# Slot sums as 512-column matmuls over four token blocks, joined by one small matmul, and a phase rounded by an integer write, in a three-layer attention and soft-MoE kernel

## The chip, the cores and the metric

The kernel runs on one core of a Trainium2 chip. The metric is the device time of one execution in microseconds. A core has TensorE (PE in the profile; its weight loads are PEld), VectorE (DVE), ScalarE (ACT), GpSimd (POOL) and SyncE (SP), which here only issues DMAs. Each engine works through its own instructions in the order in which they were written.

## What is computed

Three layers follow one another. The first is an attention with a 12 by 12 mix of the heads before and after the softmax. The second is `g = h * cos(h)` of `h = x @ w_in`, followed by `g @ w_out`. The third is a soft mixture of experts with 32 slots. The change touches the second layer and the place where it meets the third:

```python
h = x @ w_in                      # x 1792x768, w_in 768x2048
g = h * np.cos(h)
x = g @ w_out                     # never formed by the kernel
logits = x @ phi                  # 1792x32
d = np.exp(logits - logits.max(0)); d /= d.sum(0) + 1e-09
slot_input = d.T @ x              # 32x768
...                               # experts on slot_input, 8 x (768x1024, 1024x768)
c = softmax over slots; out = c @ slot_out
```

The kernel never forms `x` of the third layer. It sums `d.T @ g` (32 slots by 2048 features) and multiplies that sum by `w_out`.

## The kernel before, in words

`phase_a` is the attention, in the order that a planner writes; the change leaves it as it is. `phase_b` is the second layer and the sums over tokens, `phase_c` the experts and the output.

`phase_b` takes the 1792 tokens in four blocks of 512, 512, 512 and 256 (called blocks 0 to 3), and in each block 16 steps of 128 features, 64 steps `v` in all. The function `body(v)` writes one step. `l1` (L699 to L709) puts 18 matmuls on PE that make `h` of 128 features by 512 (or 256) tokens in one of three PSUM buffers. `act` (L716) makes the phase: ACT computes `h / 2 pi + MAGIC` (L718, an Identity with a bias tile, so that the fraction is rounded away), DVE takes MAGIC off again (L719), subtracts the whole turns from `h / 2 pi` (L720), and clears the sign (L722). `split_w` (L647 to L651) divides the weights of a later step in a high part (ACT, L649) and a low part (DVE, L650). Two steps late, `consume` (L738) turns `g` in blocks of 32 by 32 on DVE (L741) into the buffer `gn_all`, and `logits` (L743) puts four matmuls on PE every fourth step. `act2` (L726) is the sine on ACT (L727) and the product on DVE (L728). `load_w` (L640) loads the weights four steps ahead from SP's queue; in block 3 loads for the experts (`ahead`) stand between them in the same queue.

After a block, `soft` (L882) writes the block's share of the softmax into the steps of the next one: `soft0` (L753) copies the logits out, `soft1` (L758) finds the maximum and the exponentials, `soft1_turn` (L783) turns these 32 by 32 into `et`, `soft2` (L787) makes the softmax over slots, and `slots` (L801) adds `d.T @ g`. For every 32 tokens and each half of the features `slots` puts four matmuls on PE, one for each 32 rows `a` of the partitions; each reads 32 rows and 256 columns and writes 32 rows and 256 columns of one of four PSUM buffers `p` (tag "tr"). Four more accumulations stand beside each other in the 32-row strips `c` of each buffer (two for even and odd tokens in each half). A block of 512 tokens takes 128 such matmuls (256 instructions, as an f32 matmul is two), block 3 takes 64. DVE then adds the four buffers to `g_acc` (L818 in block 0, L820 later). For blocks 0 to 2 this stands in the steps of the next block, for block 3 after the last step, where `busy(n)` puts small matmuls without a use between.

`phase_c` begins with `g_acc` [128 by 1024]: 16 matmuls with stacked identities (L997) add the 32-row strips and turn the sum, ACT and DVE copy it to `gT` (L1003, L1001), and 32 matmuls `si` (L1008) multiply it by `w_out`. Then the first expert's matmuls start (`eh`, L1048). 64 units of expert weights of 768 KB go through a ring of 26 buffers: SP issues the load of a later unit when an earlier one has been used (L947). Units 0 to 17 come early; the next ones wait until the steps, `slots` of block 3 and `si` leave their buffers.

Of the kernel before, what the change touches and what calls it, by code (L numbers as in the profile page):

```python
# [9 lines left out]
F32 = mybir.dt.float32  # L10
F32R = mybir.dt.float32r
U32 = mybir.dt.uint32
AF = mybir.ActivationFunctionType
# [586 lines left out]
def phase_b(tc, st, consts, ident, xT_d, w_in, w_out, phi, sums, room, x0, ahead):  # L600
# [9 lines left out]
    with ExitStack() as ctx:  # L610
# [105 lines left out]
        def act(v, h):  # L716
            r = work(v)
            nc.scalar.activation(out=r, in_=h, func=AF.Identity, scale=INV2PI, bias=magic)  # L718
            nc.vector.tensor_scalar(out=r, in0=r, scalar1=MAGIC, scalar2=None, op0=ALU.subtract)  # L719
            nc.vector.scalar_tensor_tensor(out=r, in0=h, scalar=INV2PI, in1=r,  # L720
                                           op0=ALU.mult, op1=ALU.subtract)
            nc.vector.tensor_scalar(out=r.bitcast(U32), in0=r.bitcast(U32), scalar1=0x7FFFFFFF, scalar2=None,  # L722
                                    op0=ALU.bitwise_and)
            return h, r
# [4 lines left out]

        def gn(b, fb):  # L730
            if b == NB - 1:
                x = gn_all[:, 8192 + 1024 * fb:9216 + 1024 * fb]
            else:
                i = (4 * (b + 2 - NB) + fb) % 6
                x = gn_all[:, 2048 * i:2048 * i + 2048]
            return x
# [14 lines left out]
        et, al_t, l4_t = {}, {}, {}  # L751
# [49 lines left out]
        def slots(b):  # L801
            n = SIZES[b]
            pts = [p1.tile([128, 512], F32, tag="tr", bufs=4, name=f"p{b}_{a}")[:, :256] for a in range(4)]
            i = (4 * (b + 2 - NB)) % 6
            for t in range(n // 32):
                for half in range(2):
                    c = 2 * half + t % 2
                    x = 8192 + 2048 * half if b == NB - 1 else 2048 * ((i + 2 * half) % 6)
                    g = gn_all[:, x:x + 8 * n].rearrange("p (f t j) -> p t f j", f=8, j=32)
                    for a in range(4):  # L810
                        r = slice(32 * a, 32 * a + 32)
                        nc.tensor.matmul(pts[a][32 * c:32 * c + 32], et[b][r, 32 * t:32 * t + 32], g[r, t],  # L812
                                         start=(t < 2), stop=(t >= n // 32 - 2))
            out = g_acc.rearrange("p (f a j) -> p a f j", a=4, j=32)
            for a in range(4):
                p = pts[a].rearrange("p (f j) -> p f j", j=32)
                if b == 0:
                    nc.vector.tensor_copy(out=out[:, a], in_=p)  # L818
                else:
                    nc.vector.scalar_tensor_tensor(out=out[:, a], in0=out[:, a], scalar=al_t[b][:, 3:4],  # L820
                                                   in1=p, op0=ALU.mult, op1=ALU.add)
# [60 lines left out]
        def soft(v):  # L882
# [8 lines left out]
            elif b > 0 and f == (3 if b + 1 < NB else 4):  # L891
                slots(b - 1)

# [23 lines left out]
        slots(NB - 1)  # L917
        busy(4)
# [31 lines left out]
def phase_c(tc, ident, cT, g_acc, z_acc, gn_all, x1, cg, w1, w2, st, wo, early, gu, rest, free_x0, out):  # L950
# [5 lines left out]
    with ExitStack() as ctx:  # L956
# [36 lines left out]
        for half in range(2):  # L993
            pt = p1.tile([128, 512], F32, tag="tr", name=f"gtr{half}")
            r = slice(64 * half, 64 * half + 64)
            for k in range(8):
                nc.tensor.matmul(pt[:, 32 * k:32 * k + 32], g_acc[r, 128 * k:128 * k + 128], st[r, :32],  # L997
                                 start=True, stop=True)
            pg = pt[:, :256].rearrange("p (k s) -> p k s", s=32)
            if half:  # L1000
                nc.vector.tensor_copy(out=gT[:, 8:], in_=pg)  # L1001
            else:
                nc.scalar.copy(out=gT[:, :8], in_=pg)  # L1003
# [152 lines left out]
def tile_kernel(ctx: ExitStack, tc: tile.TileContext, q, k, v, w_pre, w_post, w_in, w_out, phi, w1, w2, out):  # L1156
# [4 lines left out]
    with tc.manual_schedule():  # L1161
# [39 lines left out]
        sums.append(pool.tile([128, w_in.shape[1] // 2], F32, name="g_acc"))  # L1201
# [51 lines left out]
```

## Time and profile before

| | us |
|---|---|
| median of 3 runs (range) | 930.11 (929.28 to 931.38) |
| the profiled execution's own time | 931.67 |
| its span | 929.8 |
| PE busy in the span | 874.4 (94%) |
| DVE busy | 643.2 (69%) |
| ACT busy | 521.0 (56%) |
| attention, until the first `h` matmul of PE's long run | 0 to 505 |
| the 64 steps of `phase_b`, first `h` matmul to last | 505 to 806 |
| end of `phase_b` to the first expert matmul | 806 to 832.5 |
| experts and output | 832.5 to 930 |

PE's 94% is a mean of stages with different limits. It holds small matmuls that wait for one another as well as full ones, and in the experts' stage the matmuls wait for weights. So what a change is worth has to be read in its own stage. The granted clock was full in `phase_b`, and between 0.5 and 0.8 of it in some stretches after.

### The profile page before, as it was taken

What the parts mean: (1) busy time and instruction counts of PE and PEld (TensorE: products, weight loads), DVE (VectorE), ACT (ScalarE), POOL (GpSimd) and SP (SyncE); (2) the same over time, 40 slices, a digit from 0 to 9 for tenths busy, and PEclk for the clock granted to TensorE, in tenths of its full rate; (3) what the DMA queues carried; (4) which work ended last, traced back from release to release, by engine and by line L of the source; (5) the groups of instructions that cost most, each with busy time, mean ns of one, the idle gap of its engine ahead of it and who ended that gap; (6) DMA issues with size and microseconds to landing.
All of it is one profiled execution on the core that took longest, in us unless ns stands there. A gap on an engine that the chain in (4) does not pass through costs nothing.

```text
span 929.8 us, 18916 instructions
## 1 busy us (share of the span) xinstructions
PE 874.4 (94%) x7176; PEld 623.6 (67%) x7176; DVE 643.2 (69%) x1348; ACT 521.0 (56%) x1139; POOL 178.8 (19%) x272
## 2 busy tenths in 40 slices
PE   7898999999999999999999999999998989889765
PEld 5556777776777777777778877777776767753212
DVE  4566887778779778778744777887877888823003
ACT  5565777677767678666655644564554546502002
POOL 3232443433434334343300000000000000010000
PEclk9999999999999999999999999999999999989768
DMA  7999797999788997979327732463553467969998
GB/s 166 184 200 216 194 239 214 200 229 261 224 206 224 222 241 180 249 203 248 102 88 249 230 120 68 160 213 110 182 182 126 139 215 215 315 252 414 417 374 291
DMA packets 175478, 198.99 MB, mean 214 GB/s; under 512 B 73424, under 2 KB 147090, under 8 KB 175388
## 3 DMA queue, kind: packets, MB, share of 16 engines
q1 hardware_dynamic: 158504, 159.18, 57.9%
q0 software_dynamic: 14272, 37.96, 18.1%
q8 instruction: 57, 0.93, 0.5%
q10 hardware_dynamic: 2612, 0.65, 0.3%
q14 instruction: 33, 0.27, 0.1%
HBM read 135.40 MB, written 23.59 MB: 171 GB/s over the span
## 4 chain that ended last, share of the span: by engine, by line
PE 75%; DMA 11%; DVE 6%; SPq 3%; ACT 2%; issue 2%; POOL 0%; ACTq 0%; POOLq 0%; DVEq 0%
PE po L443 15%; PE pre L405 14%; PE av L467 8%; PE h L705 7%; PE s L358 7%; PE h L706 7%; PE h L708 7%; DMA early<-in_moe_w_dram 3%; DMA knat<-in_k_dram 3%; PE p L812 2%; DMA cg<-in_moe_w_dram 2%; DMA ring<-in_moe_w_dram 2%; DVE wf L650 2%; PE eh L1048 1%; DMA s<-ss 1%
## 5 line engine op out<-in xcount | busy, mean ns | idle before, releaser
L443 PEld LDWEIGHTS po<-wc,e 120*112 120x112 f32 x1440 | 171.4, 178 | 56.2 <-issue 41.6
L443 PE MATMUL po<-wc,e 120*112 120x120 f32 x1440 | 183.5, 269 | 0.5 <-ACT am L228 0.5
L405 PE MATMUL pre<-s,kron_pre 120*120 120x448 f32 x360 | 168.3, 558 | 5.8 <-issue 3.7
L408 DVE TENSOR_REDUCE mz<-pre 120x1 f32<-120x448 f32 x180 | 111.0, 620 | 49.9 <-PE pre L405 49.0
L378 POOL DMA_DIRECT2D s<-ss x180 | 107.1, 597 | 181.9 <-ACT ss L228 135.5
L705 PE MATMUL h<-x,wh 128*128 128x512 f32 (+1 forms) x384 | 138.7, 371 | 1.3 <-ACT wh L649 1.3
L706 PE MATMUL h<-x,wh 128*128 128x512 f32 (+1 forms) x384 | 135.5, 363 | 0.0
L412 ACT ACTIVATE e<-pre,mz 120x448 f32<-120x448 f32 x180 | 114.5, 637 | 30.8 <-DVE mz L408 28.1
L228 ACT COPY am<-po 112x360 f32<-112x360 f32 x190 | 87.3, 461 | 65.4 <-PE po L443 63.3
L705 PEld LDWEIGHTS h<-x,wh 128*128 128x128 f32 x384 | 72.1, 188 | 24.2 <-ACT cg L718 5.9
L708 PE MATMUL h<-x,wf 128*128 128x512 f32 (+1 forms) x384 | 87.5, 363 | 0.0
L542 POOL TENSOR_TENSOR nar<-nar,cvt 128x384 uint32<-128x384 uint32 x64 | 64.0, 1000 | 98.7 <-DVE cvt L533 42.7
L467 PE MATMUL av<-am,v 112*64 112x120 f32 (+1 forms) x1536 | 83.0, 262 | 0.0
L718 ACT ACTIVATE cg<-h,consts 128x512 f32<-128x512 f32 (+1 forms) x64 | 40.2, 629 | 75.0 <-PE h L708 73.9
L467 PEld LDWEIGHTS av<-am,v 112*64 112x64 f32 x1536 | 74.0, 137 | 10.4 <-issue 5.2
L706 PEld LDWEIGHTS h<-x,wh 128*128 128x128 f32 x384 | 72.2, 188 | 11.3
L708 PEld LDWEIGHTS h<-x,wf 128*128 128x128 f32 x384 | 66.2, 188 | 12.0
L727 ACT ACTIVATE cg<-cg,consts 128x512 f32<-128x512 f32 (+1 forms) x64 | 42.9, 671 | 49.0 <-DVE cg L722 48.8
L1022 POOL MEMSET own<- 128x192 f32 x2 | 0.4, 252 | 361.4 <-PE si L1008 361.4
L405 PEld LDWEIGHTS pre<-s,kron_pre 120*120 120x120 f32 x360 | 54.0, 186 | 23.2 <-issue 17.5
L228 ACT COPY ss<-s 120x448 f32<-120x448 f32 (+1 forms) x104 | 54.1, 532 | 24.9 <-PE s L358 15.6
L650 DVE TENSOR_TENSOR wf<-wf,wh 128x768 fp32r<-128x768 f32 x64 | 60.9, 951 | 9.1 <-ACT wh L649 9.1
(171 smaller groups left out, 1252.8 us busy)
## 6 DMA issues: line engine op xcount, KB each, us to landing
s<-ss POOLq DMA_DIRECT2D x144, 210.0 KB, 7.5
early<-in_moe_w_dram SPq DMA_DIRECT2D x36, 768.0 KB
wf<-w SPq DMA_DIRECT2D x64, 384.0 KB
raw<-in_moe_w_in_dram SPq DMA_DIRECT2D x32, 384.0 KB
w<-nar SPq DMA_DIRECT2D x64, 192.0 KB
raw<-in_moe_w_out_dram SPq DMA_DIRECT2D x32, 384.0 KB
gn<-in_moe_w_dram SPq DMA_DIRECT2D x16, 768.0 KB
early<-w SPq DMA_DIRECT2D x8, 768.0 KB
```

What stands on the lines that cost most here:

```text
L228: nc.scalar.copy(out=out, in_=in_)
L358: nc.tensor.matmul(pts[o][:n, :S], x[r, p, :n], y[r, p, :], start=(i == 0), stop=(i == 2))
L378: QUEUE[e].dma_start(out=s2t[ti][h::12, :n // 10], in_=x[o][:n])
L405: nc.tensor.matmul(prt[gi, c][:, :S], kpre, s2t[ti][:, 3 * g + c, :], start=True, stop=True)
L408: nc.vector.tensor_reduce(out=mz[gi][:, 0, c:c + 1], in_=prt[gi, c][:, :S], axis=AX.X, op=ALU.max, negate=True)
L412: nc.scalar.activation(out=et[gi][:, c, :], in_=prt.pop((gi, c))[:, :S], func=AF.Exp, bias=mz[gi][:, 0, c:c + 1], accum_out=mz[gi][:, 1, c ...
L443: nc.tensor.matmul(pt[:, :360].rearrange("p (g i) -> p g i", i=30)[:, :, 10 * c:10 * c + 10], et[gi][:, c, jt * CJ:(jt + 1) * CJ], wct[gi] ...
L467: nc.tensor.matmul(pt[64 * o:64 * o + 64, x * 120:x * 120 + n], vt[:, g, jt, :], am[ti % 2][:, g, jt, :n], start=(jt == 0), stop=(jt == NJ ...
L650: nc.vector.tensor_tensor(out=wf_t[v], in0=wf_t[v].bitcast(F32), in1=wh.bitcast(F32), op=ALU.subtract)
L705: nc.tensor.matmul(pt, wh[:, c], xh[:, c, :], start=(c == 0), stop=False)
L706: nc.tensor.matmul(pt, wh[:, c], xl[:, c, :], start=False, stop=False)
L708: nc.tensor.matmul(pt, wl[:, c], xh[:, c, :], start=False, stop=(c == 5))
```

## The change

It does four things. The added rows push later code down: L720 of the changed kernel is L718 of the one before, and so on.

1. `act`: ACT multiplies by `1 / 2 pi` and writes a 32-bit integer (Copy, no bias tile). The subtraction on DVE reads that integer, and the instruction that took MAGIC off is gone.
2. `slots`: one matmul covers all 16 x 32 features (512 columns) of its 32 rows, and the strips `c` are four token blocks. A block of 512 tokens takes 64 matmuls, block 3 takes 32. The four full buffers are copied to scratch columns of `gn_all` (block 3: the last one to `cg`), two by ACT, two by DVE.
3. `slots_sum`, new: four matmuls with stacked identities add the strips of each buffer; DVE adds the result to `g_acc`, now [128 by 512], in one instruction (two in block 3). It stands two steps after `slots`; after block 3 right behind it, with four more small matmuls `busy(4)`.
4. `phase_c`: two 32 by 32 turns on DVE make `gT` from `g_acc`. The 16 matmuls and the two copies are gone.

The buffers of `gn` are laid out anew (`HALVES`), so that `slots` can read 16 x 32 features with one pattern.

```diff
         def act(v, h):
             r = work(v)
-            nc.scalar.activation(out=r, in_=h, func=AF.Identity, scale=INV2PI, bias=magic)
-            nc.vector.tensor_scalar(out=r, in0=r, scalar1=MAGIC, scalar2=None, op0=ALU.subtract)
-            nc.vector.scalar_tensor_tensor(out=r, in0=h, scalar=INV2PI, in1=r,
+            i = r.bitcast(I32)
+            nc.scalar.activation(out=i, in_=h, func=AF.Copy, scale=INV2PI)
+            nc.vector.scalar_tensor_tensor(out=r, in0=h, scalar=INV2PI, in1=i,
                                            op0=ALU.mult, op1=ALU.subtract)
...
+        HALVES = [(0, 2), (1, 2), (0, 1)]
+
         def gn(b, fb):
             if b == NB - 1:
-                x = gn_all[:, 8192 + 1024 * fb:9216 + 1024 * fb]
+                return gn_all[:, 8192 + 1024 * fb:9216 + 1024 * fb]
+            x = 4096 * HALVES[b][fb // 2] + 2048 * (fb % 2)
+            return gn_all[:, x:x + 2048]
...
         def slots(b):
             n = SIZES[b]
-            pts = [p1.tile([128, 512], F32, tag="tr", bufs=4, name=f"p{b}_{a}")[:, :256] for a in range(4)]
-            i = (4 * (b + 2 - NB)) % 6
+            pts = [p1.tile([128, 512], F32, tag="tr", bufs=4, name=f"p{b}_{a}") for a in range(4)]
+            g = all_gn(b)
             for t in range(n // 32):
-                for half in range(2):
-                    c = 2 * half + t % 2
-                    x = 8192 + 2048 * half if b == NB - 1 else 2048 * ((i + 2 * half) % 6)
-                    g = gn_all[:, x:x + 8 * n].rearrange("p (f t j) -> p t f j", f=8, j=32)
-                    for a in range(4):
-                        r = slice(32 * a, 32 * a + 32)
-                        nc.tensor.matmul(pts[a][32 * c:32 * c + 32], et[b][r, 32 * t:32 * t + 32], g[r, t],
-                                         start=(t < 2), stop=(t >= n // 32 - 2))
-            out = g_acc.rearrange("p (f a j) -> p a f j", a=4, j=32)
+                c = 32 * (t % 4)
+                for a in range(4):
+                    r = slice(32 * a, 32 * a + 32)
+                    nc.tensor.matmul(pts[a][c:c + 32], et[b][r, 32 * t:32 * t + 32], g[r, t],
+                                     start=(t < 4), stop=(t >= n // 32 - 4))
+            if b + 1 < NB:
+                sc = gn(b, 3)
+                sc_t[b] = [sc[:, 512 * a:512 * a + 512] for a in range(4)]
+            else:
+                sc_t[b] = [gn_all[:, 10752 + 512 * a:11264 + 512 * a] for a in range(3)] + [cg[:, :512]]
             for a in range(4):
-                p = pts[a].rearrange("p (f j) -> p f j", j=32)
-                if b == 0:
-                    nc.vector.tensor_copy(out=out[:, a], in_=p)
+                if a % 2:
+                    nc.vector.tensor_copy(out=sc_t[b][a], in_=pts[a])
                 else:
-                    nc.vector.scalar_tensor_tensor(out=out[:, a], in0=out[:, a], scalar=al_t[b][:, 3:4],
-                                                   in1=p, op0=ALU.mult, op1=ALU.add)
+                    nc.scalar.copy(out=sc_t[b][a], in_=pts[a])
+
+        def slots_sum(b):
+            pt = p1.tile([128, 512], F32, tag="tr", bufs=4, name=f"ps{b}")
+            for a in range(4):
+                nc.tensor.matmul(pt[32 * a:32 * a + 32], st[:, :32], sc_t[b][a], start=True, stop=True)
+            if b == 0:
+                nc.vector.tensor_copy(out=g_acc, in_=pt)
+            else:
+                for c in (slice(0, 512),) if b + 1 < NB else (slice(0, 256), slice(256, 512)):
+                    nc.vector.scalar_tensor_tensor(out=g_acc[:, c], in0=g_acc[:, c], scalar=al_t[b][:, 3:4],
+                                                   in1=pt[:, c], op0=ALU.mult, op1=ALU.add)
...
             elif b > 0 and f == (3 if b + 1 < NB else 4):
                 slots(b - 1)
+            elif b > 0 and f == (5 if b + 1 < NB else 6):
+                slots_sum(b - 1)
...
         slots(NB - 1)
         busy(4)
+        slots_sum(NB - 1)
+        busy(4)
...
         for half in range(2):
-            pt = p1.tile([128, 512], F32, tag="tr", name=f"gtr{half}")
-            r = slice(64 * half, 64 * half + 64)
-            for k in range(8):
-                nc.tensor.matmul(pt[:, 32 * k:32 * k + 32], g_acc[r, 128 * k:128 * k + 128], st[r, :32],
-                                 start=True, stop=True)
-            pg = pt[:, :256].rearrange("p (k s) -> p k s", s=32)
-            if half:
-                nc.vector.tensor_copy(out=gT[:, 8:], in_=pg)
-            else:
-                nc.scalar.copy(out=gT[:, :8], in_=pg)
+            nc.vector.transpose(out=gT[:, 8 * half:8 * half + 8].rearrange("p k s -> p (k s)"),
+                                in_=g_acc[:, 256 * half:256 * half + 256])
```

The order of the instructions changes in three places that matter here. The first is a step of block 3 on DVE. Before, from one turn of `g` to the next:

```order
L741 STREAM_TRANSPOSE gn<-cg 128x256
L728 TENSOR_TENSOR cg<-h_8468,cg 128x256
L719 TENSOR_SCALAR cg<-cg 128x256
L720 SCALAR_TENSOR_TENSOR cg<-h_8498,cg 128x256
L722 TENSOR_SCALAR cg<-cg 128x256
L650 TENSOR_TENSOR wf_5880<-wf_5880,wh_5884 128x768
```

Now, at the same place of DVE's order:

```order
L750 STREAM_TRANSPOSE gn<-cg 128x256
L729 TENSOR_TENSOR cg<-h_8236,cg 128x256
L721 SCALAR_TENSOR_TENSOR cg<-h_8265,cg 128x256
L723 TENSOR_SCALAR cg<-cg 128x256
L651 TENSOR_TENSOR wf_5880<-wf_5880,wh_5884 128x768
```

Five instructions stand where six stood, in all 64 steps. The second place is PE after the last `slots`. Before:

```order
L812 MATMUL p_3_8701<-gn,cg 32x256
L899 MATMUL idle<-ident 128x128 x4
L997 MATMUL gtr_8805<-st,g_acc 128x32 x8
L997 MATMUL gtr_8815<-st,g_acc 128x32 x8
L1008 MATMUL si_8825<-x_5972,gT 32x384 x4
```

Now, on PE from the last `slots` to the first `si`:

```order
L818 MATMUL p_3_8463<-gn,cg 32x512
L920 MATMUL idle<-ident 128x128 x4
L834 MATMUL ps_8504<-gn,st 32x512 x3
L834 MATMUL ps_8504<-cg,st 32x512
L920 MATMUL idle<-ident 128x128 x4
L1023 MATMUL si_8548<-x_5972,gT 32x384 x4
```

The sixteen `gtr` are replaced by four `ps` and four more small ones. The third place is DVE at the same point. Before:

```order
L820 SCALAR_TENSOR_TENSOR g_acc<-g_acc,m_8672,p_0_8698 128x8x32
L820 SCALAR_TENSOR_TENSOR g_acc<-g_acc,m_8672,p_1_8699 128x8x32
L820 SCALAR_TENSOR_TENSOR g_acc<-g_acc,m_8672,p_2_8700 128x8x32
L820 SCALAR_TENSOR_TENSOR g_acc<-g_acc,m_8672,p_3_8701 128x8x32
L991 TENSOR_SCALAR rz<-z_acc 128x1
L992 RECIPROCAL rz<-rz 128x1
L1001 COPY gT<-gtr_8815 128x256
```

Now, on DVE up to the turns that `si` waits for:

```order
L827 COPY gn<-p_1_8461 128x512
L827 COPY cg<-p_3_8463 128x512
L839 SCALAR_TENSOR_TENSOR g_acc<-g_acc,m_8434,ps_8504 128x256 x2
L1014 TENSOR_SCALAR rz<-z_acc 128x1
L1015 RECIPROCAL rz<-rz 128x1
L1017 STREAM_TRANSPOSE gT<-g_acc 128x256 x2
```

DVE now works twice between `slots` and `si`: on the copies ahead of the `ps` matmuls, and on the sums and turns behind them. POOL's and SP's order are as before.

## Rows read from the trace of the kernel before

**Rows 1.** Windows: stretch, its length, each engine's busy us (instructions), clock, DMA.

```profile
636.00:686.00 50.00, 50.00 (x225) 37.80 (x225) 44.44 (x73) 27.04 (x38) 0.00 (x0) 1.00 0.57 186
...
786.00:797.00 11.00, 10.30 (x92) 9.57 (x91) 9.49 (x25) 6.31 (x12) 0.00 (x0) 1.00 0.94 304
797.00:806.00 9.00, 9.00 (x79) 8.37 (x80) 8.79 (x22) 5.47 (x11) 0.00 (x0) 1.00 0.95 302
...
824.00:826.00 2.00, 2.00 (x16) 0.61 (x19) 0.42 (x1) 0.00 (x0) 0.00 (x0) 0.50 1.01 421
...
828.00:830.00 2.00, 2.00 (x32) 0.75 (x28) 0.00 (x0) 0.00 (x0) 0.00 (x0) 1.00 0.03 8
...
846.00:870.00 24.00, 22.65 (x184) 9.47 (x176) 6.19 (x16) 4.74 (x12) 0.39 (x3) 0.93 1.02 415
```

**Rows 2.** Chain that ended last, in block 1: start us, us, what.

```profile
638.08 1.40 PE h L708 x6
642.28 1.40 PE h L708 x6
```

**Rows 3.** Timeline of PE: `slots` of blocks 0, 1, 2: start, us, line, [idle before].

```profile
624.45 5.17 PE L812 MATMUL p<-gn 32*32 32x256 f32 x242 [0.38 <-DVE gn L785]
630.24 0.66 PE L812 MATMUL p<-gn 32*32 32x256 f32 x14 [0.62 <-issue]
...
705.06 3.41 PE L812 MATMUL p<-gn 32*32 32x256 f32 x163 [1.03 <-DVE gn L785]
710.13 2.10 PE L812 MATMUL p<-gn 32*32 32x256 f32 x93 [1.66 <-issue]
...
778.53 4.04 PE L812 MATMUL p<-gn 32*32 32x256 f32 x195 [0.20 <-DVE gn L785]
783.50 1.47 PE L812 MATMUL p<-gn 32*32 32x256 f32 x61 [0.93 <-issue]
```

**Rows 4.** Timeline of DVE, one step of block 3.

```profile
797.70 0.44 DVE L741 STREAM_TRANSPOSE gn<-cg 128x256 f32<-128x256 f32 x1
...
798.07 0.39 DVE L728 TENSOR_TENSOR cg<-h,cg 128x256 f32<-128x256 f32 x1
...
798.37 0.27 DVE L719 TENSOR_SCALAR cg<-cg 128x256 f32<-128x256 f32 x1
...
798.68 0.42 DVE L720 SCALAR_TENSOR_TENSOR cg<-h,cg 128x256 f32<-128x256 f32 x1
...
800.22 0.44 DVE L741 STREAM_TRANSPOSE gn<-cg 128x256 f32<-128x256 f32 x1
```

**Rows 5.** Timeline of DVE behind `slots` of block 2.

```profile
785.33 1.64 DVE L820 SCALAR_TENSOR_TENSOR g_acc<-g_acc,m,p 128x256 f32<-128x256 f32 x4
787.75 0.29 DVE L719 TENSOR_SCALAR cg<-cg 128x256 f32<-128x256 f32 x1 [0.79 <-ACT cg L718]
```

**Rows 6.** Chain, the step of block 3 that waited for its weights.

```profile
789.28 6.61 DMA wf<-w
```

**Rows 7.** Chain from the last `slots` to the experts.

```profile
814.43 2.79 PE p L812 x115
817.22 1.64 DVE g_acc L820 x4
...
818.93 5.20 PE gtr L997 x32
824.14 6.06 PE si L1008 x56
```

**Rows 8.** Timeline of PE: the four `logits` matmuls of 512 columns, two instructions each.

```profile
623.00 1.06 PE L748 MATMUL lg<-cg,wphi 128*32 128x512 f32 x8
```

**Rows 9.** Groups by line and form, 500 to 835 us: busy us, mean ns.

```profile
L719 DVE TENSOR_SCALAR cg<-cg 128x512 f32<-128x512 f32 x48 | 20.4, 424 | 40.0 <-ACT cg L718 40.0
...
L674 DVE COPY early<-wtr 128x512 f32<-128x512 f32 x12 | 7.8, 680 | 0.0
...
L676 ACT COPY early<-wtr 128x512 f32<-128x512 f32 x12 | 6.9, 587 | 1.8 <-PE wtr L671 1.8
```

**Rows 10.** Timeline of DVE: one of the two small operations on `rz`.

```profile
818.96 0.16 DVE L992 RECIPROCAL rz<-rz 128x1 f32<-128x1 f32 x1
```

More of the change, by code (lines that the diff above doesn't have):

```diff
@@ L12 @@
 U32 = mybir.dt.uint32
+I32 = mybir.dt.int32
 AF = mybir.ActivationFunctionType
@@ L728, in act2, with all_gn @@
             nc.vector.tensor_tensor(out=r, in0=h, in1=r, op=ALU.mult)
+        HALVES = [(0, 2), (1, 2), (0, 1)]
         def gn(b, fb):
             if b == NB - 1:
-                x = gn_all[:, 8192 + 1024 * fb:9216 + 1024 * fb]
-            else:
-                i = (4 * (b + 2 - NB) + fb) % 6
-                x = gn_all[:, 2048 * i:2048 * i + 2048]
-            return x
+                return gn_all[:, 8192 + 1024 * fb:9216 + 1024 * fb]
+            x = 4096 * HALVES[b][fb // 2] + 2048 * (fb % 2)
+            return gn_all[:, x:x + 2048]
+        def all_gn(b):
+            if b == NB - 1:
+                x = gn_all[:, 8192:].rearrange("p (h x) -> p h x", h=2)
+            else:
+                i, j = HALVES[b]
+                x = gn_all.rearrange("p (h x) -> p h x", h=3)[:, i:j + 1:j - i]
+            return x.rearrange("p h (f t j) -> p t h f j", f=8, j=32)
         def consume(v, g):
@@ L749, in logits @@
                                  start=(f == 3), stop=(f == 15))
-        et, al_t, l4_t = {}, {}, {}
+        et, al_t, l4_t, sc_t = {}, {}, {}, {}
         def soft0(b):
@@ L1200, in tile_kernel @@
         sums.append(pool.tile([128, B * S // 128, 32], F32, name="cT"))
-        sums.append(pool.tile([128, w_in.shape[1] // 2], F32, name="g_acc"))
+        sums.append(pool.tile([128, w_in.shape[1] // 4], F32, name="g_acc"))
         sums.append(pool.tile([128, 1], F32, name="z_acc"))
```

## The prediction

> **What bounds the kernel now.** I read the windows by stage first. In block 1, from 636 to 686 us, PE is busy all 50.0 us and DVE 44.4 [rows 1]; the chain shows one step of 18 matmuls every 4.20 us (642.28 less 638.08) [rows 2]. Blocks 0 to 2 are PE's, then, and DVE has some 0.46 us to spare in a step (5.6 us over 12 steps). In block 3 (797 to 806) PE looks as busy, 9.0 of 9 us, but its matmuls have half the columns, so a step needs only about 2.1 us of it. The timeline of DVE shows what sets the pace there: its instructions start before the one ahead of them ends, and a turn of `g` follows the last after 2.52 us (797.70, 800.22) [rows 4]. The DMA engines are close behind, at 0.94 and 0.95 of their time from 786 to 806 [rows 1], and one step did wait for its weights [rows 6]. From the last `slots` on the chain is serial: 2.79 us of `slots`, DVE's sums, 5.20 us of `gtr`, then `si` [rows 7]. Lastly I looked at what comes after. From 846 the DMA engines run at 1.02 of their time with 415 GB/s, and weights set the end. But between 828 and 830 they stand at 0.03 [rows 1]: the next buffers come free only with `si` and the first expert. So whatever makes `si` earlier makes the whole stream of weights earlier, one for one, until that hole is closed.
>
> **The change, part by part.**
>
> *The phase.* One DVE instruction less in each of 64 steps. In blocks 0 to 2 that is 0.42 us a step [rows 9] on an engine that isn't the bound: nothing, except where PE waits for DVE. It waits 0.38 and 1.03 us for the turned exponentials ahead of `slots` of blocks 0 and 1 [rows 3]. Four steps of the DVE work before that turn lose 0.42 each, 1.7 together, more than either wait: **-1.4**. In block 3 DVE is the path, and an instruction costs the distance of two starts, 0.31 (798.37 to 798.68) [rows 4]; I take 0.30 by 16 steps: **-4.8**. ACT's instruction changes from an Identity to a Copy, and ACT has 23 of 50 us idle in block 1 [rows 1]; I cost it at nothing, and it would have to grow by more than 1 us a step to matter. What no row shows is a subtraction that reads an integer beside a float. The bounds are the present 0.42 [rows 4] and twice that; I take the present, since its columns, its buffers and its engine stay.
>
> *The matmuls of `slots`.* They now take 6.45 us in block 0 (624.45 to 630.90), 7.17 in block 1 and 6.44 in block 2; 0.62, 1.66 and 0.93 of that are holes in which PE waited for nothing but its own instructions [rows 3]. The 256 instructions become 128 with twice the columns. Columns times rows stay the same, so the only gain is in overlap and in these holes. The lower bound comes from the logits: four matmuls of 512 columns in four strips beside each other take 1.06 us with the pipeline's fill and drain [rows 8], which I estimate at 0.2. If four row groups run beside them as well, 64 matmuls are four such rounds, 3.4 to 4.2 us. The upper bound is no better overlap than now: 7.17 less its hole, 5.5. I take **4.0**, near the logits, because half the instructions leave PE's queue half as often empty. That is -2.45 in block 0 and -3.17 in block 1, on the path. In block 2 it counts little: DVE is the path there, and DVE lost only 0.79 us behind it, waiting for ACT, that waited for `h` [rows 5]: **-0.8**. Block 3's own goes from 2.79 [rows 7] to 2.1: **-0.7**.
>
> *Copies and the joining matmuls.* Each block gets four more matmuls like the logits, 1.06 with their drain, 1.1 with the change of tile shape: **+2.2** on PE for blocks 0 and 1; block 2's lies in block 3, where PE has room. DVE's four sums of 1.64 [rows 5] become two copies of 0.68 [rows 9], 1.3 as they overlap by a little, and one sum of 512 columns, about 0.6: +0.25 of DVE, covered in blocks 0 and 1 by its spare time, on the path in block 3. ACT's two copies of 0.59 [rows 9] lie in time in which it waited for `h`. If that cover were gone they would cost 1.2 a block.
>
> A rule speaks against this part. The row first: the two copies on each engine take 1.2 to 1.3 us a block [rows 9], and in blocks 0 and 1 the next user of the four buffers is the joining matmul two steps, 8.4 us [rows 2], later; so they are hidden. The Trainium skill (TensorEngine Tiling (Array Packing), PSUM Bottleneck) says that tiling speeds up the array but not the reading out of PSUM, which can become the bound. By it the sum would be smaller by 2.6, two blocks of 1.3; by the rows it stands. It is the fifth rival.
>
> Block 3 together: -4.8 - 0.8 + 0.25 = -5.35. I give back 0.4, since weights that arrive just in time now [rows 1, 6] will be late sooner: **-4.9**.
>
> *The end.* From the end of `slots` to `si` it is now 6.92 us (817.22 to 824.14) [rows 7]. Then: two DVE copies 1.3, ACT's two beside them; the last joining matmul, alone on PE, 1.0 [rows 8]; two sums of 256 columns, 0.41 each as now [rows 7], 0.8; two small operations of 0.16 [rows 10], 0.3; the first turn, 0.44 as for `g` [rows 4]; four hand-overs between engines, under 0.1 each, 0.25 in all. That is 4.1: **-2.8**. The second turn is hidden behind the first `si`. I leave `si` at its 6.06.
>
> The sum: -1.4 - 2.45 - 3.17 + 2.2 = -4.8 in blocks 0 to 2; -4.9 in block 3; -0.7 - 2.8 = -3.5 at the end; **-13.2**. Does the hole in the DMAs hold that? Four units of 768 KB wait for the last `slots`, 1.9 us each at 415 GB/s [rows 1], 7.6 us. Two now wait for the joining matmuls instead, whose scratch lies in them. `si` ends some 10 us after `slots` (4.1 and 6.06), so a hole of 1 to 2 us remains. The profiled execution took 931.67 us, 1.9 over its span and 1.6 over the median of 930.11; the same gain from the median gives 916.9. I say **917**.
>
> **The rivals.**
>
> 1. *No better overlap.* `slots` stays at 5.5 without holes: +1.5 in each of blocks 0 and 1 and +0.7 in block 3, **920.6**. For it: sixteen places are used now too. Against: the holes of "issue" [rows 3] say that instructions are short, not columns. Chance 0.10.
> 2. *Weights bind block 3.* From 786 to 806 the DMA engines have 1.1 us of 20 left [rows 1]; the forecast takes some 3 us out of that stretch: +2, **919**. For it: the wait of rows 6. Against: a wait for DMA ended only in one step. It would show as longer waits of `wh` for `wf`. Chance 0.12.
> 3. *The slow clock in `si`.* At 824 to 826 the granted clock is 0.50, at 828 to 830 it is 1.00, with 16 and 32 matmul instructions in 2 us [rows 1]. The dense 5.20 us of `gtr` are gone, and PE now waits for DVE twice before `si`. At half clock throughout, its 64 instructions need 8 to 10 us: up to +4, **921**; at full clock throughout -1. Chance 0.10.
> 4. *The mixed subtraction takes twice as long.* 0.42 more in 16 steps of block 3, while blocks 0 to 2 can cover it: +6.7, **923.7**. Chance 0.03.
> 5. *Reading out PSUM binds*, the rule above: +2.6, **919.5**. Chance 0.04.
> 6. *Slower: four at a time.* If 512 columns let the row groups no longer run beside each other (each reads its own 32 partitions and writes its own buffer), 64 matmuls are sixteen rounds of 1.06 [rows 8], 17 us a block: +13 in each of blocks 0 and 1, +6 in block 3, **949**. It decides from a round of sixteen of 2.3 us on: ten rounds lie on the path, and 13.2 over ten added to 1.0 is that. Against: now eight rounds of sixteen take 5.5 to 5.8 us [rows 3], 0.7 each, on the same sixteen places. Chance 0.03.
>
> Several of rivals 1 to 4 at once could eat nearly all of it, so that less than 0.2% (1.9 us, about what a measurement of this kernel can tell from no change) is left: chance 0.03. The forecast itself has 0.55.
>
> **How the numbers follow.** Faster: 0.55 and rivals 1 to 5, 0.94. Same 0.03, slower 0.03. The range: below, `slots` at 3.4 (-1.5), `si` at full clock (-1), nothing given back for weights (-0.4), and as much again for waits that I don't see, some -5; above, rivals 1 to 3 two at a time, +7. That is 911.5 to 924, and leaves out rival 6, the case of no change, and combinations of more.
>
> **What would show it.** `slots` of blocks 0 and 1 at 3.4 to 4.5 us without holes; PE's wait ahead of it gone; a step of block 3 at about 2.2 us on DVE; no subtraction longer there than 0.43; the last `slots` some 10 us earlier; 4.1 us from its end to `si`; a hole of DMA near the end of `si`, then the same stream as before. The prediction is wrong if the stream of weights begins 13 us earlier and the end doesn't, if block 3 keeps steps of 2.5 us, or if the joining matmuls or copies make `h` wait.

## The result and the profile after

| | before | changed |
|---|---|---|
| median, us (range, runs) | 929.69 (928.84 to 931.38, 4) | 914.91 (911.71 to 919.98, 4) |
| ratio of the two, 95% interval | | 0.9856 (0.9819 to 0.9893) |
| profiled execution, us | 931.67 | 911.71 |
| its span, us | 929.8 | 909.9 |
| DVE busy in the span, us | 643.2 | 620.6 |

By the medians the change makes the kernel 14.8 us faster; 917 with a range of 911.5 to 924 had been forecast. Two later series gave ratios of 0.9866 (0.9822 to 0.9911) and 0.9882 (0.9848 to 0.9915). Over the three series the gain is 11 to 15 us, 1.2 to 1.4% by the ratios, and no interval reaches 1; the 13.2 of the forecast lies in the middle.

The two profiled spans differ by 19.9 us, which is more than the medians do. So the first thing to read is where in the span the difference lies. The start times in the timeline of PE cut it in five stages. The second column for each kernel is a later profile of the same program:

| stage, us | before | before, again | changed | changed, again | changed, third |
|---|---|---|---|---|---|
| start to first `h` (attention) | 505.4 | 503.4 | 498.0 | 498.7 | 502.2 |
| blocks 0 to 2, first `h` to first `h` of block 3 | 250.2 | 250.1 | 246.3 | 246.3 | 246.3 |
| block 3, to the start of its `slots` | 58.9 | 61.0 | 53.5 | 55.5 | 56.5 |
| `slots` of block 3 to the first `eh` | 18.1 | 18.2 | 13.5 | 13.5 | 13.5 |
| first `eh` to the end | 97.3 | 97.0 | 98.5 | 98.6 | 98.5 |

Three rows repeat to within 0.3 us in each profile of a program; two do not. The attention, whose code is the same in both kernels, spreads by 4 us between profiles of one program, and block 3 by 2 to 3. What the change does has to be read from rows that repeat, from profiles in the same state, or from medians.

The `slots` of blocks 0 and 1 and the joining matmuls, timeline of PE of the changed kernel (start us, us, line, idle time before; it answers to [rows 3]):

```profile
616.60 4.46 PE L818 MATMUL p<-gn 32*32 32x512 f32 x128
...
629.58 1.06 PE L834 MATMUL ps<-gn,st 128*32 128x512 f32 x8
...
695.27 4.46 PE L818 MATMUL p<-gn 32*32 32x512 f32 x128
```

The 128 instructions stand in one piece, without a hole inside and without a wait ahead of them. Each block now takes 4.46 us, where it took 6.45 and 7.17. The joining matmuls show no wait either.

One step of DVE in block 3, its timeline (it answers to [rows 4]), and the two instructions of the phase in the page's list of groups (busy us, mean ns):

```profile
784.44 0.44 DVE L750 STREAM_TRANSPOSE gn<-cg 128x256 f32<-128x256 f32 x1
784.80 0.38 DVE L729 TENSOR_TENSOR cg<-h,cg 128x256 f32<-128x256 f32 x1
785.11 0.41 DVE L721 SCALAR_TENSOR_TENSOR cg<-h,cg 128x256 f32<-128x256 f32 x1
785.55 0.29 DVE L723 TENSOR_SCALAR cg<-cg 128x256 uint32<-128x256 uint32 x1
785.76 0.95 DVE L651 TENSOR_TENSOR wf<-wf,wh 128x768 fp32r<-128x768 f32 x1
786.63 0.44 DVE L750 STREAM_TRANSPOSE gn<-cg 128x256 f32<-128x256 f32 x1
```

```profile
L720 ACT ACTIVATE cg<-h 128x512 int32<-128x512 f32 (+1 forms) x64 | 34.6, 541 | 90.7 <-PE h L709 89.5
...
L721 DVE SCALAR_TENSOR_TENSOR cg<-h,cg 128x512 f32<-128x512 f32 (+1 forms) x64 | 39.8, 621 | 57.2 <-ACT cg L720 55.2
```

The step is 2.19 us (784.44 to 786.63), where it was 2.52, and the subtraction that reads an integer takes 0.41, where it took 0.42 with two floats.

The chain of waits of the changed kernel in that stretch (start us, us, what) shows that in this profile DVE is then no longer what the end waits for:

```profile
773.45 0.68 PE h L709 x6
774.13 0.99 PE ps L834 x8
...
781.55 0.68 PE h L709 x6
783.59 0.68 PE h L709 x6
785.63 0.68 PE h L709 x6
786.31 0.57 PE lg L757 x8
```

From 764 to 791 us every piece of it is on PE: a step of `h` every 2.04 us (781.55, 783.59, 785.63), the logits, and the joining matmuls of block 2 with 0.99. Before, the chain behind `slots` of block 2 held two such steps of PE, then a load of weights of 6.61 us [rows 6], and from there to the end of the block DVE. DVE is not far behind in the changed kernel: from 772 to 791 it is idle for no more than 1.1 us. And the shown profile is not the usual one: in eight of the eleven profiles with the new end (`after`, `e2_slots` and `e10_room` are the others) the chain of block 3 goes through a load of weights of 5 to 7 us. `e8_room` has one of 5.01 us, with DVE behind it, and takes the same 53.5 us. PE, DVE and the weights are close to one another in this block.

From the last `slots` to the experts, timeline of PE (it answers to [rows 7]):

```profile
797.82 2.35 PE L818 MATMUL p<-gn,cg 32*32 32x512 f32 x64 [1.27 <-DVE cg L794]
800.10 0.66 PE L920 MATMUL idle<-ident 128*128 128x128 f32 x4
800.89 1.15 PE L834 MATMUL ps<-gn,st 128*32 128x512 f32 x5
...
802.58 0.66 PE L920 MATMUL idle<-ident 128*128 128x128 f32 x4
804.26 5.37 PE L1023 MATMUL si<-x,gT 128*32 128x384 f32 x64 [1.03 <-issue]
```

`slots` ends at 800.17, and `si` begins 4.1 us later, as forecast. `si` itself takes 5.37 us, where it was left at its old length. The windows show why, and also something that had not been foreseen (stretch, its length, busy us of PE, PEld, DVE, ACT and POOL with instructions, clock, DMA share, GB/s; they answer to [rows 1]):

```profile
798.00:800.00 2.00, 2.00 (x64) 0.64 (x44) 0.90 (x5) 0.26 (x1) 0.00 (x0) 1.00 0.63 253
800.00:802.00 2.00, 1.86 (x21) 0.94 (x12) 1.29 (x2) 1.07 (x2) 0.00 (x0) 1.00 0.08 34
802.00:804.00 2.00, 1.23 (x8) 0.42 (x4) 1.28 (x5) 0.00 (x0) 0.00 (x0) 1.00 0.00 0
804.00:806.00 2.00, 1.74 (x24) 0.94 (x28) 0.48 (x2) 0.00 (x0) 0.00 (x0) 1.00 0.65 135
806.00:808.00 2.00, 2.00 (x32) 0.97 (x27) 0.00 (x0) 0.00 (x0) 0.00 (x0) 1.00 1.01 406
```

The clock is 1.00 all through `si`, where it was 0.50 in part. But the DMA engines stand still from 800 to 804, before `si` even starts, where a hole near its end was forecast. The timeline of SP's queue and SP's waits from 770 to 830 (us in total, times, longest) name the cause:

```profile
791.59 2.74 SPq L1230 DMA_DIRECT2D x<-w  x4
803.70 0.33 SPq L970 DMA_DIRECT2D ring<-in_moe_w_dram  x1
804.13 1.54 SPq L970 DMA_DIRECT2D gn<-in_moe_w_dram  x3
```

```profile
SPq L970 <- DVE g_acc L839: 9.2, 1, 9.2
```

SP waited 9.2 us for the very last sum on DVE (L839) before it issued the load of unit 20 into the third `ring` buffer. In the kernel before that load left at 810.73, ahead of the last `slots` at 814.43, and the `gn` loads at their end (SP's timeline of the kernel before):

```profile
810.73 0.33 SPq L947 DMA_DIRECT2D ring<-in_moe_w_dram  x1
817.15 1.64 SPq L947 DMA_DIRECT2D gn<-in_moe_w_dram  x3
```

The explanation that an experiment below tests: the change halves the tile of `g_acc`, the pools behind it move by 2 KB, and this buffer comes to lie over a tile that the last sum still reads, probably one of the softmax's small ones. Behind it in SP's queue stand the three `gn` units, of which `slots` had set the first free some 4 us earlier.

### The profile page after: what moved, and what is told of

It is laid out like the page before. It is cut to its first block, busy times and chain, and to the rows that moved or that the text cites. A ratio compares the mean times of both kernels' runs of the same rounds, so it can differ in the third digit from the quotient of the medians.

```text
span 909.9 us, 17966 instructions
## 1 busy us (share of the span) xinstructions
PE 866.6 (95%) x6732; PEld 612.4 (67%) x6732; DVE 620.6 (68%) x1282; ACT 519.4 (57%) x1146; POOL 178.8 (20%) x272
## 4 chain that ended last, share of the span: by engine, by line
PE 81%; DMA 11%; DVE 2%; SPq 1%; issue 1%; ACT 1%; POOL 0%; ACTq 0%; DVEq 0%; POOLq 0%
PE po L444 16%; PE pre L406 15%; PE h L706 9%; PE av L468 8%; PE h L707 8%; PE h L709 8%; PE s L359 8%; DMA early<-in_moe_w_dram 4%; DMA s<-ss 4%; PE p L818 2%; DMA cg<-in_moe_w_dram 2%; DMA ring<-in_moe_w_dram 2%; PE lg L757 1%; PE kt L293 1%; PE wtr L672 1%
## 5 line engine op out<-in xcount | busy, mean ns | idle before, releaser
L720 ACT ACTIVATE cg<-h 128x512 int32<-128x512 f32 (+1 forms) x64 | 34.6, 541 | 90.7 <-PE h L709 89.5
L721 DVE SCALAR_TENSOR_TENSOR cg<-h,cg 128x512 f32<-128x512 f32 (+1 forms) x64 | 39.8, 621 | 57.2 <-ACT cg L720 55.2
L709 PEld LDWEIGHTS h<-x,wf 128*128 128x128 f32 x384 | 66.3, 188 | 11.8
```

The lines of the kernel that those rows point to most:

```text
L709: nc.tensor.matmul(pt, wl[:, c], xh[:, c, :], start=False, stop=(c == 5))
```

## Experiments

### The two parts apart

`e1_phase` is the kernel before with the integer phase alone, `e2_slots` the changed kernel with the old phase. The first of these edits (the second undoes the same lines):

```diff
-            nc.scalar.activation(out=r, in_=h, func=AF.Identity, scale=INV2PI, bias=magic)
-            nc.vector.tensor_scalar(out=r, in0=r, scalar1=MAGIC, scalar2=None, op0=ALU.subtract)
-            nc.vector.scalar_tensor_tensor(out=r, in0=h, scalar=INV2PI, in1=r,
+            i = r.bitcast(I32)
+            nc.scalar.activation(out=i, in_=h, func=AF.Copy, scale=INV2PI)
+            nc.vector.scalar_tensor_tensor(out=r, in0=h, scalar=INV2PI, in1=i,
```

> The kernel before with the phase alone changed: ACT writes the integer, DVE's removal of MAGIC is gone; slots, sums and turns are the old ones. By the sum: both waits ahead of slots in blocks 0 and 1 gone (-1.4), 16 DVE instructions of 0.30 in block 3 (-4.8), of which about 0.6 comes back since DVE reaches the end of slots of block 2 sooner and waits there: -5 to -6 in all. Rival (DVE's subtraction with an integer is slower, or weights bind block 3): -3 or less, with longer waits of wh for wf in block 3.

> The changed kernel with the old phase: ACT adds MAGIC, DVE takes it off; slots, the joining matmuls and the turns are the new ones. By the sum of the parts: blocks 0 and 1 -3.6 (slots -6.0, joining +2.4), the end -4.5 (chain -3.2, si at full clock -1.3), block 3 -0.5, and the load of unit 20 still waits for the last sum (+1 to +2): -7 to -9 in all. Rival: the parts need each other (slots are faster only because DVE is ahead): less than -5.

Measured, each over 12 runs against a kernel before of 931.85: the phase alone 926.37 (ratio 0.9945, 0.9909 to 0.9981), `slots` alone 923.59 (0.9916, 0.9888 to 0.9944). That is 5.5 and 8.3 us, both inside what was expected, and the sum of 13.8 is close to what both together gave (14.1 in the same series, 917.76). So the parts add as far as these intervals of some 3 us to either side can tell, and both are clear of no change. The term for PE's waits ahead of `slots` belongs to the phase, as its working said: in `e2_slots` they are still there, in the changed kernel they are gone. Timeline of PE in `e2_slots`:

```profile
618.63 4.46 PE L818 MATMUL p<-gn 32*32 32x512 f32 x128 [0.39 <-DVE gn L794]
...
698.47 4.46 PE L818 MATMUL p<-gn 32*32 32x512 f32 x128 [1.07 <-DVE gn L794]
```

And `e1_phase`, which keeps the 256 short instructions, shows the largest hole of all; its `slots` of block 1 took 9.7 us from start to end:

```profile
702.18 3.40 PE L813 MATMUL p<-gn 32*32 32x256 f32 x163
...
708.51 1.96 PE L813 MATMUL p<-gn 32*32 32x256 f32 x50 [2.92 <-issue]
```

Behind that hole the granted clock fell as well, to 0.57 and 0.58 on average in the windows from 708 to 712. So in this profile blocks 0 to 2 took 251.5 us, 1.3 more than before, although both waits ahead of `slots` are gone from it: the holes in `slots` grew by more than the waits had cost. Whether that is chance or belongs to the phase alone, one profile doesn't tell.

### The price of a round of sixteen

`slots` took 4.46 us where 4.0 was forecast, and 2.35 after block 3 where 2.1 was. `e6_half` keeps the 128 instructions and halves their columns (the copies' edit isn't shown):

```diff
-                    nc.tensor.matmul(pts[a][c:c + 32], et[b][r, 32 * t:32 * t + 32], g[r, t],
+                    nc.tensor.matmul(pts[a][c:c + 32, :256], et[b][r, 32 * t:32 * t + 32], g[r, t, 0],
```

> The changed kernel with 256 columns in each slots matmul in place of 512: it leaves out half of the features of the sums (the copies take each half twice, so that they keep their size). It prices a round of sixteen matmuls. Theory 1: a round has a fixed part of some 0.2 us beside its columns: 0.63 a round, so slots takes 2.8 us in blocks 0 to 2 and 1.5 in block 3. Theory 2: the price goes by columns, half of 1.06: 2.35 and 1.3. On the holes: if they come with short instructions in close order, they are back (over 3.1 us in a block); if with 256 instructions in one stretch, there are none with these 128. The end comes earlier by about twice the 1.7 us of one block, by 3 to 5.

Timeline of PE in `e6_half`, blocks 0 and 3:

```profile
622.79 2.76 PE L818 MATMUL p<-gn 32*32 32x256 f32 x128
...
799.71 1.49 PE L818 MATMUL p<-gn,cg 32*32 32x256 f32 x64 [1.28 <-DVE cg L794]
```

Theory 1, to a few hundredths. Four rounds less two are 1.27 us, so a round of 256 columns is 0.635; with 512 columns it is (4.46 - 2.35) / 2 = 1.055. Columns make 0.42 of the difference for each 256, so some 0.21 us of every round doesn't depend on columns, and a start and end of 0.2 comes once. Four rounds in place of eight save 4 x 0.21, a little under 1 us a block; the rest of the 2.0 and 2.7 us that a block gained is holes and smaller gaps. There was no hole in this kernel, though its instructions are as short as those of before. Short instructions alone don't make the hole, then.

The place of the holes says more. In both profiles of before and in `e1_phase` they came behind the same number of instructions, 242 in block 0, 163 in block 1 and 195 in block 2; only their lengths differ, 0.56 to 2.92 us. The traces also hold the packets of a queue of instructions, q8 (the pages of before and of the changed kernel: packets, MB, share of 16 engines):

```profile
q8 instruction: 57, 0.93, 0.5%
...
q8 instruction: 53, 0.87, 0.4%
```

The packets go with PE's 7176 and 6732 matmuls, one packet of 16 KB for 126 or 127 of them. In all nine holes PE began again 1.27 to 1.43 us after such a packet had landed: in block 1 of `e1_phase` the packet landed at 707.13 and PE went on at 708.51. So the holes are most likely PE waiting for its own instructions, of which 256 short matmuls in one stretch use up as many as two packets bring and 128 only one. That is read from times that agree; no run changed the loading of instructions.

The execution of `e6_half` took 912.68 us in a single run.

### The wait of SP's queue

```diff
-        sums.append(pool.tile([128, w_in.shape[1] // 4], F32, name="g_acc"))
+        sums.append(pool.tile([128, w_in.shape[1] // 2], F32, name="g_acc")[:, :512])
```

> The changed kernel once more, as the mark for the other runs. The first profile of it began its first long run of h matmuls at 500.4 us, that of the kernel before at 505.4, though the attention ahead of it is the same code. Theory: that is chance, and the gain of the change is 13 to 16 us (914 to 917), with the first h matmul anywhere from 500 to 507. Rival: the change gains in the attention too, by the place of its buffers; then the first h matmul is at 500 to 501 again and at 505 or later in every kernel with the old layout.

> The changed kernel, with the tile of g_acc as large as before and only its first half used. That moves the ring of weights back by 2 KB in every partition, so that buffer ring2 no longer lies over the small tile whose scalar the last sum reads. In the changed kernel the load of unit 20 (ring2) was issued at 803.70, behind the last sum, and held four loads behind it in SP's queue, while the DMA engines stood at 0.04 from 800 to 804 us. Theory: that wait costs part of the gain; without it the loads of units 20 to 24 start up to 12 us (unit 20) and 3.5 us (21, 22) earlier, the stream behind them by 2.5 to 3, and the time is 2 to 3 us under the changed kernel. Rival: the stream is bound by when the first expert starts, which doesn't move: no difference (under 1 us).

> The changed kernel again, beside the next one. Some 915 to 918 us.

> The kernel of e3_room again (the tile of g_acc kept at its old size, so that the ring buffer of unit 20 no longer lies over the small tiles of the softmax), now beside the changed kernel in one series. Theory 1: the hole of 5 us in the DMAs was paid one for one, and the half of it that goes makes the kernel 2 to 3 us faster. Theory 2: it is given back, since the weights end no earlier (95.1 us from the start of the last slots against 95.8 and 95.4 in two profiles without it): 0 to 1 us.

The wait went. Timeline of SP's queue in `e8_room`:

```profile
790.81 3.19 SPq L1230 DMA_DIRECT2D x<-w  x4
794.11 0.43 SPq L970 DMA_DIRECT2D ring<-in_moe_w_dram  x1
799.47 2.54 SPq L970 DMA_DIRECT2D gn<-in_moe_w_dram  x3
```

The third `ring` load leaves before the last `slots`, the `gn` loads at its end. So does most of the hole; windows of `e3_room`, whose last `slots` start at 801.41:

```profile
804.00:806.00 2.00, 1.86 (x12) 0.63 (x10) 1.14 (x2) 0.92 (x2) 0.00 (x0) 1.00 0.79 230
806.00:808.00 2.00, 0.97 (x10) 0.59 (x12) 1.69 (x6) 0.00 (x0) 0.00 (x0) 1.00 0.84 338
...
812.00:816.00 4.00, 3.50 (x34) 1.66 (x30) 2.12 (x7) 0.58 (x1) 2.20 (x3) 1.00 0.87 324
816.00:820.00 4.00, 4.00 (x42) 1.17 (x36) 0.52 (x3) 0.00 (x0) 0.33 (x3) 1.00 0.67 189
```

A second hole now stands behind the first, at 812 to 820, where the queue waits for the buffers that `si` and the first expert give back. Counted as the share that is missing to 1.00, the changed kernel lost some 5.3 us from 798 to 806, this one 0.7 and 1.8 in the two places. (The kernel before lost 6.9, from 816 to 818 and from 826 to 836.) The medians were 915.07 beside 917.76 in the first series and 916.35 beside 919.15 in the second, 2.7 and 2.8 us less. The ratios to the kernel before differ by less: 0.9845 (0.9806 to 0.9885) beside 0.9866 is 2.0 us, 0.9878 (0.9829 to 0.9927) beside 0.9882 only 0.4, and the intervals overlap in both series. In the profiles the stage from the first `eh` to the end is shorter by 0.6 to 0.8 us (97.9 and 97.7 beside 98.6 and 98.5 in the same series), and a third profile of this kernel, `e10_room` below, has 97.1, as the kernel before. So it is shown that the wait came from where the buffer lies, that the hole is not paid one for one, and that the end gives back 0.6 us or more; whether the time of the whole kernel gains 2 to 3 us these runs don't settle.

### The clock in `si`

In the three profiles with `gtr` the granted clock falls to 0.50, the lower of its two levels, while `gtr` runs, and stays there into `si`, which took 6.7 us in the first profile of before, 8.1 in the second and 8.2 in `e1_phase`. In all eleven profiles with the new end it took 5.37, at a clock of 1.00. The new end has eight small matmuls without a use around the joining ones, which might be what keeps the clock:

```diff
         slots(NB - 1)
-        busy(4)
         slots_sum(NB - 1)
-        busy(4)
```

> The changed kernel without the eight small matmuls around the joining matmuls after block 3. Theory 1: the clock in si is full because the serial small matmuls of before (gtr, 5.2 us of weight loads) are gone, and the fillers do nothing: si again 5.4 us at a granted clock of 1.00. Theory 2: the fillers hold the clock: without them some of si runs at 0.50, and it takes 6.7 to 8.2 us as in the kernels with gtr; the first expert matmuls and the stream of weights come later by as much, 1.3 to 2.9 us.

Windows of `e5_quiet` from the end of `slots` into `si`:

```profile
810.00:812.00 2.00, 0.41 (x2) 0.01 (x1) 1.52 (x6) 0.00 (x0) 0.00 (x0) 1.00 0.00 0
812.00:814.00 2.00, 1.98 (x28) 1.00 (x31) 0.24 (x1) 0.00 (x0) 0.00 (x0) 1.00 0.72 190
814.00:816.00 2.00, 2.00 (x32) 1.01 (x28) 0.00 (x0) 0.00 (x0) 0.00 (x0) 1.00 0.99 412
```

PE is busy only 0.41 of 2.00 us before `si`, and the clock stays at 1.00; `si` again took 5.37, and began 6.44 us after the start of `slots` as in the changed kernel. The fillers do nothing here in this one profile (a single run of 919.54 us, beside 931.59 for the kernel before). What went with `gtr` is the clock's fall: it came in three of three profiles with it and in none of eleven without.

### What scatters between executions

> The kernel before, profiled once more, for the attention, whose code is the same in all kernels: its first h matmul started at 505.4 us in the profile of before, at 498.0 and 498.7 in two profiles of the changed kernel, at 499.6 to 503.7 in the others. Theory 1: chance in the first loads; this profile may start h anywhere from 498 to 505, and from h to the end it again takes 424 us. Theory 2: the program before is slow there by itself (its buffers lie elsewhere): again 505, and then some 5 of the 20 us between the two profiles were won in the attention.

Its first `h` came at 503.4 (in a single run of 931.47 us), the third profile of the changed kernel had it at 502.2, `e8_room` at 497.2 and `e6_half` at 504.2. (The 500.4 in the expectation for the second series of the changed kernel is a later `h` matmul of that profile; its first is at 498.0.) That speaks for theory 1, chance: the eleven profiles with the new end, whose attention is the same code, spread over 7 us. The spread begins in the first 100 us, where PE waits 2.1 to 6.2 us in total for the first loads of `k`. The three profiles with the old layout, 503.4 to 505.4, still lie in the upper part of it; whether they are slower there by some 3 us on average so few can't tell. From the first `h` to the end it took 426.3 (424.4 in the first profile), the changed kernel 411.9, 413.9 and 414.8. That is 11.8 us between the means, without the attention.

The spread of block 3 showed a clock as well. Windows of the third profile of the changed kernel, `e7_after`, where block 3 took 56.5 us:

```profile
756.00:758.00 2.00, 0.17 (x2) 0.00 (x0) 2.00 (x5) 1.27 (x3) 0.00 (x0) 1.00 1.00 324
758.00:760.00 2.00, 1.93 (x7) 1.39 (x8) 1.97 (x6) 0.51 (x1) 0.00 (x0) 0.74 1.07 387
760.00:762.00 2.00, 2.00 (x10) 2.00 (x11) 1.16 (x4) 0.93 (x1) 0.00 (x0) 0.50 1.12 333
762.00:764.00 2.00, 2.00 (x11) 2.00 (x10) 0.28 (x2) 1.32 (x4) 0.00 (x0) 0.50 0.81 290
764.00:766.00 2.00, 2.00 (x12) 2.00 (x12) 0.67 (x2) 1.10 (x2) 0.00 (x0) 0.55 0.07 27
```

PE stands still from 756 to 758, waiting 1.9 us for DVE's copy of the logits, and then the clock falls to 0.50 for some 7 us. In the first profile the same wait is there (0.10 us busy from 752 to 754), and the clock stays at 1.00. Over the twelve profiles with this wait, of whatever kernel, the clock fell behind it in six. `e9_fill` is `e8_room` with the wait filled:

```diff
+            pt = p1.tile([128, 512], F32, tag="tr", bufs=4, name=f"lt{b}")
+            for _ in range(14 if b == NB - 2 else 0):
+                nc.tensor.transpose(pt[:, :128], ident, ident)
             lg = p2.tile([128, 512], F32, tag="lg", name=f"lgsum{b}")[:, :n]
             nc.tensor.matmul(lg, st, l4, start=True, stop=True)
-            pt = p1.tile([128, 512], F32, tag="tr", bufs=4, name=f"lt{b}")
```

> The kernel of e8_room with 14 small matmuls without a use on TensorE, ahead of the first of the sum of logits (lgsum) after block 2, where it waits 1.9 us for the copied logits in every profile of the changed kernel. In some profiles the granted clock is 0.50 for some 7 us behind that wait (block 3 then takes 56.5 us from its first h to the last slots), in others not (53.5). Theory 1: the wait brings the clock down; with it filled, block 3 takes 53.5 us at a full clock, the stage from the first h to the end 411 us, and the mean is 1 to 2 us below that of e10_room. Theory 2: the clock falls for another reason: it falls here as well in half of the executions, and the fillers cost up to 0.3 us.

> The kernel of e8_room again, beside the one with fillers: 915 to 916 us, 53.5 or 56.5 us in block 3 by the clock.

> The kernel of e9_fill once more. Its one profile had a full clock in block 3, which chance gives in half of the executions. Theory 1: full again at the start of block 3 (a granted clock of 1.00 in all stretches of 2 us behind the sum of logits), 53.5 to 54 us to the last slots, 411 from the first h to the end, some 915 us. Theory 2: a clock of 0.50 there in this profile, 56 us.

`e9_fill` took 915.59 us (ratio 0.9824, 0.9778 to 0.9871) beside 918.97 for `e10_room` (0.9855, 0.9812 to 0.9897), with intervals that overlap, and 912.93 as `e11_fill` (0.9808, 0.9775 to 0.9842) in a series of its own. Windows of `e11_fill` at the same place, its wait being down to 0.37 us:

```profile
758.00:760.00 2.00, 1.63 (x14) 1.39 (x13) 2.00 (x5) 1.01 (x2) 0.00 (x0) 1.00 1.08 334
760.00:762.00 2.00, 2.00 (x14) 1.52 (x14) 1.97 (x6) 0.51 (x1) 0.00 (x0) 1.00 1.03 374
762.00:764.00 2.00, 2.00 (x20) 2.00 (x19) 0.86 (x3) 1.22 (x1) 0.00 (x0) 1.00 1.12 343
```

Both profiles with fillers kept the full clock and took 53.9 and 53.6 us in block 3; `e10_room` lost the clock (0.50 from 758 to 760) and took 54.7. With one in two as the rate, two in a row without a fall come by chance one time in four, so the mechanism is likely, not shown. The kernel with both edits has the lowest ratios: it is 1.8 and 1.9% faster than the kernel before, where the changed kernel is 1.2 to 1.4%. No series has these two side by side.

## Why the prediction was right, and where its terms were off

**Blocks 0 to 2, -4.8 forecast, -3.9 in the profiles** (250.2 to 246.3). The waits ahead of `slots` went, as said. `slots` was sized at 4.0 and takes 4.46: the step that failed is "four such rounds", taken from the logits with an estimated start and end of 0.2 that counted only once. Each round has its own 0.21. So block 0 gained 1.99 and block 1 2.71, in place of 2.45 and 3.17. A joining sum lengthens its step by about 1.2, not 1.1: in the changed kernel 5.39 us in place of 4.20 [rows 2]. That half the instructions would leave PE's queue less often empty was borne out: all three holes are gone.

**Block 3, -4.9 forecast; -5.4 between the first two profiles, which have a full clock there, and -4.5 between the second of before and the third of changed, which both have the fall to 0.50** (58.9 to 53.5, 61.0 to 56.5). That a DVE instruction costs 0.30 a step was right (2.52 to 2.19), and so was that the integer operand costs nothing. That sixteen of these lie on the path was wrong for the second half: in the profile shown PE took over there, with 2.04 us a step, 0.57 for each group of logits and 0.99 for the joining matmuls that the forecast had called free ("where PE has room"). How much of the block's gain is the phase's stays open: `e2_slots`, with the old phase and the same fall of the clock, took 59.0, which would leave it 2.5 in place of 4.8, but that is one profile. The weights, rival 2, cost something in some profiles: the second one of the changed kernel has a load of `wf` of 7.09 us on its chain, and took 55.5, at a full clock. That is the 2 us more that the rival had named.

**The end, -3.5 forecast, -4.6 in every profile** (18.1 to 13.5). `slots` gave 0.4, not 0.7 (2.76 to 2.35); from its end to `si` came out at 4.1, step by step as worked out; `si` gave another 1.35 (6.72 to 5.37) that the sum had left out, with "I leave `si` at its 6.06". The second profile of before divides the same 4.6 otherwise, since its clock fell later: 5.5 us from `slots` to `si` and 8.1 of `si`. So a part of the 2.8 is the clock's fall in `gtr`, which the sum took for the chain's own length. Rival 3 had asked in which direction its clock goes; the answer is the better of its two cases, "at full clock throughout -1".

**The hole, 0 forecast, +1.2** (97.3 to 98.5 from the first `eh` to the end). The sentences that failed are "Four units of 768 KB wait for the last `slots`" and "Two now wait for the joining matmuls instead": all four waited, in the order of SP's queue, for the last sum on DVE. Nothing in the prediction said where buffers come to lie when a tile shrinks. With the buffer moved back the stage took 97.9, 97.7 and 97.1, so this wait had from half of the 1.2 to all of it.

The sum by stages is -3.9 - 5.4 - 4.6 + 1.2 = -12.7 between the first two profiles without the attention (12.5 before rounding), beside -13.2 forecast. That it came so close is luck in part, as errors cancelled: 0.9 too much in blocks 0 to 2 and 1.2 for the hole against 1.1 too little at the end and 0.5 in block 3. The other 7.4 us between these profiles lie in the attention, most of it chance as far as the fourteen profiles of all kernels tell.

**The other rivals.** No better overlap (1): a round of 512 columns at 1.055 costs less than two of 256 at 0.635, so there is some. The weights (2) and the clock in `si` (3) are told above. Twice as long a subtraction (4) and four at a time (6) are out by 0.41 us and 1.055 us. Reading out PSUM (5): the four copies took 0.57 to 0.69 us each on ACT and DVE and no joining matmul in blocks 0 to 2 waited for one. The rule of the Trainium skill behind that rival (TensorEngine Tiling (Array Packing), section PSUM Bottleneck), by which the read-out can become the bound, did not decide here; after block 3, where the copies do lie on the path, their time was in the 4.1.

## What to carry to other kernels

A matmul in small tiles has a price per round beside its columns; get it from two sizes in the trace before forecasting what fewer, longer instructions bring. When a tile is made smaller, look at which buffers move with it and what each DMA issue then waits for: here one late load held the four behind it in its queue. When an engine has holes without a wait for another, see whether they come at the same instruction each time, and what the queue of instructions does then. And before a difference of two profiles is explained, profile each program again: here 4 us of attention and 2 to 3 us of a lower clock came and went with no change in the code.

## What the runs showed of the hardware that was not expected

- A round of sixteen 32 by 32 tiles took 0.635 us at 256 columns and 1.055 at 512, so 0.21 of each did not depend on the columns.
- 256 matmul instructions in one stretch had a hole of 0.56 to 2.92 us in nine of nine cases, in each block at the same instruction in three profiles (behind 242, 163 and 195). Each ended 1.27 to 1.43 us after a packet of 16 KB had landed in the queue of instructions. 128 in one stretch had none, at 256 columns as at 512.
- A vector operation with a 32-bit integer beside a float took as long as with two floats (0.41 and 0.42 us at 256 columns).
- Behind the same wait of 1.9 to 2.9 us of TensorE the granted clock fell to 0.50 in six profiles of twelve and stayed at 1.00 in six. Ahead of `si` it stayed at 1.00 with PE busy 0.41 of 2.00 us, and fell during the 3.9 to 5.4 us of `gtr` in which PE was busy all the time with weight loads and matmuls of 32 columns.
